# Earlier and wider spaced x sums, half-width k-v products and a split last output in a fused linear-attention and bilinear-GLU kernel

## The chip, the cores and the metric

The kernel runs on one core of one Trainium2 chip. The metric is the device time of one execution in microseconds (us). One execution was also profiled: its instructions, waits and transfers are what the profile and the trace below show. The engines are called as the profile calls them: PE (matmuls) with PEld (weight loads), DVE, ACT, POOL, and SP, whose queue issues most of the transfers.

## The reference

Two branches read the same input `x` (2048 x 512) and are mixed by a gate per row:

```python
x = A_x
g = _sigmoid((x * gate_w).sum(-1, keepdims=True))
# linear attention, 32 heads of 16, phi(t) = (t > 0 ? t + 1 : exp(t)) + 1e-6
q, k, v = split(x @ wqkv)
kv  = einsum("bhsd,bhse->bhde", phi(k), v);  z = phi(k).sum over s
a   = (einsum(phi(q), kv) / (einsum(phi(q), z) + 1e-6)) @ wo
# bilinear GLU, 1792 hidden columns
b   = ((x @ w_gate) * (x @ w_up)) @ w_down
return g * a + (1 - g) * b
```

## The kernel before, in words

**Numbers in two parts.** Every fp32 operand is split into a high part (rounded to the type fp32r) and a low part (the rest). A product is three matmuls, high x high, high x low and low x high (`mm3`, L73). The splits cost ACT (the high parts, `act`) and DVE (the low parts, `tt`) one pass each.

**First stage.** Sixteen tiles of 128 rows are turned into phi(k), and x^T phi(k) is summed in four PSUM banks (`gt`), which `g_evac` (L786) copies out as `gts`.

**Second stage.** 2048 columns of x^T are worked in two pairs of 1024 columns (`NPAIR` = 2). A pair has 16 units: two for q (`q0`, `q1`) and 14 for the GLU. The products of a unit are done with seven half-size products in place of eight (Strassen's scheme, with Winograd-like sums), so a unit is seven slots of six matmuls each; slot s of unit n has the number 7n + s, and the first unit starts at 81.4 us of the span. The seven products need sums of blocks of x (`xc`, one for each of the products 1 to 7, table `SUMS` at L166) and sums of blocks of the weights (`wr`, loaded by `w_load` through SP, added up by `w_add`: two ACT copies and an accumulating transfer issued by POOL).

**What is hung on slots.** `later(slot, fn)` puts a step behind the product of a slot, and `unit` (L649) calls in each slot: the product, the evacuations that wait, the steps of that slot, the weight steps (`side`), the seeding of the next PSUM bank, the links of the Strassen sums (`crit`), and a down-projection job. Each engine works its own instructions strictly in the order in which they were recorded, and so do the queues of SP and POOL. An instruction at the head that waits, waits for all behind it.

**The sums for the second pair.** For i = 3, 4, 1, 6, 7 and two halves k, `x_raw` (L753) loads a block of 256 KB by SP into a work buffer `xw`; `x_sum` (L757) negates it on ACT where the sum is a difference (i = 3 and 4, so four times), then adds another block by an accumulating transfer that POOL issues; `x_park` (L760) writes the sum to a scratch `xpark` in memory by SP, for which the accumulation must have landed; `x_free` (L763) gives the buffer back. At the turn between the pairs `x_turn` loads the parked sums into `xc`. Work buffers come from a list of 45, first in first out (`get`, `put`), so a change of the order of `get` also changes which buffer each later step has.

**The k-v products.** `kv_unit` (L794), in slot 16, multiplies `wv` by `gts` in plain fp32: for each of four blocks b of 128 columns, four products of 128 x 128 by 128 columns, summed in the PSUM bank `pkv`. Each such product leaves two weight loads and two matmuls in the trace. Only the 16 x 16 blocks on the diagonal are wanted: `kv_split` (L803), slot 18, multiplies the bank by a mask (`kvm`), and splits the result.

**The end of a pair.** `turn` (L975) runs eight jobs of six pieces (18 matmuls, `piece`, L958) in which the attention output and the rest of the down-projection are summed in a bank `pdn`; `done` (L945) adds the bank to the accumulator tile `M` on DVE and stores `M` in `out`. Three PSUM banks are shared in turn by these jobs. The last steps on `M` (`steps`, L584) are hung on pieces by their offset, piece p having offset 14 + p.

Of the kernel before, what the change touches and what calls it, by code (L numbers as in the profile page):

```python
# [42 lines left out]
def gated_mix(ctx: ExitStack, tc, xt, xp, x, wqkv, wq, wq_add, wo, wgu, wgu_add, wdn, wdn_add, wdl, gate_w, out):  # L43
# [6 lines left out]
    def mm(*args, **kw):  # L50
        tc.keep_in_program_order(nc.tensor.matmul(*args, **kw))  # L51
# [7 lines left out]
    def tt(dst, a, b, op):  # L59
        pin(nc.vector.tensor_tensor(dst, a, b, op=op))  # L60
# [125 lines left out]
    def get(name):  # L186
        k = spare.pop(0)
        w = p2.tile([P, CH], F32R, tag=f"w{k}", name=name)
        held[id(w)] = (k, w)
        return w  # L190
# [5 lines left out]
    def f32(w):  # L196
        return w.bitcast(F32)
# [4 lines left out]
    def job_bank():  # L202
        return bank_of("pd", "pdn", 3)
# [285 lines left out]
    class Group:  # L489
# [50 lines left out]
        def plain(self):  # L540
# [27 lines left out]
            def add(a, b, d, op, free):  # L568
                m = macc[b, d]
                tt(f32(macc[a, d]), f32(macc[a, d]), m if b == STAYS else f32(m), op)  # L570
                if free and b != STAYS:
                    put(macc.pop((b, d)))
# [11 lines left out]
            def steps(off, *fns):  # L584
                for k, fn in enumerate(fns):
                    if pair == NPAIR - 1 or off + k < 14 + TURN[0]:
                        when(min(off + k, 13 + TURN[pair]), fn)
                    else:
                        later(7 * units * (pair + 1) + (off + k - 14 - TURN[0]) // 2, fn)
# [6 lines left out]
            for d in range(2):  # L596
                steps(39 + 3 * d, lambda d=d: add(2, 4, d, ALU.add, False), lambda d=d: scale(2 + d, 0))
            for d in range(2):
                steps(50 + 6 * d, lambda d=d: add(7, 1, d, ALU.add, False), lambda d=d: add(7, 4, d, ALU.add, True),
                      lambda d=d: scale(d, 0))  # L600

        def seed(self, i, d):
# [175 lines left out]
    def wp_load():  # L778
# [4 lines left out]
        for k in range(KT):  # L783
            dma(f32(att["wo"][k]), wo[k * P:(k + 1) * P, :])

    def g_evac():  # L786
        att["g"] = [get("gts") for _ in range(KT)]
        for d in range(KT):
            if d % 2:
                act(f32(att["g"][d]), accs[d])  # L790
            else:
                pin(nc.vector.tensor_copy(f32(att["g"][d]), accs[d]))

    def kv_unit():  # L794
        pkv = psum.tile([P, KT, P], F32, tag="pd", name="pkv", bufs=3)
        for b in range(KT):
            sl = slice(b * P, (b + 1) * P)
            for d in range(KT):
                mm(pkv[:, b], f32(att["wv"][d])[:, sl], f32(att["g"][d])[:, sl], start=d == 0, stop=d == KT - 1)
        att["pkv"] = pkv  # L800
        put(*att["wv"], *att["g"])

    def kv_split():  # L803
        kvm, hi, lo = get("kvm"), get("kvh"), get("kvl")
        tt(blocks(f32(kvm)), att["pkv"], bmask[:, None, :].to_broadcast([P, KT, P]), ALU.mult)
        act(hi, f32(kvm))
        tt(lo, f32(kvm), f32(hi), ALU.subtract)
        put(kvm)
        att["kvm"] = [hi, lo]
# [131 lines left out]
    def ends_jobs(pair):  # L941

        gr = groups[pair * NG + NG - 1]

        def done(d, c, bank):  # L945
            w = c_tile(d, c)
            tt(f32(w), f32(w), bank, ALU.add)
            col = (2 * pair + c) * CH
            to = nc.gpsimd if pair == 0 else nc.sync
            pin(to.dma_start(out[d * P:(d + 1) * P, col:col + CH], f32(w)))  # L950
            if pair == 0:
                later(now_slot[0] + 8, lambda: put(w))

        for c in 1, 0:
            for n, d in enumerate(half[c]):
                box = {}

                def piece(k, c=c, n=n, d=d, box=box):  # L958
                    sl = slice(d * P, (d + 1) * P)
                    if k == 0:  # L960
                        box["bank"] = job_bank()
                    if k < KT:
                        w, h = [v[:, sl] for v in wp[k]], os_[k, c]
                    else:
                        w = [v[:, d // 2, (d % 2) * P:(d % 2 + 1) * P] for v in dcs[gr.g, k - KT + 1]]
                        h = gr.ops[("12", "22")[k - KT] if c else ("11", "21")[k - KT]]
                    mm3(box["bank"], w, h, k == 0, k == KT + 1)
                    if n == 3:
                        put(*(os_.pop((k, c)) if k < KT else h))
                    if k == KT + 1:  # L970
                        waiting.append(lambda: done(d, c, box["bank"]))

                queue.extend(lambda k=k, piece=piece: piece(k) for k in range(KT + 2))
# [25 lines left out]
    for p in range(NPAIR):  # L999
        last = 7 * (units * (p + 1) - 1)  # L1000
        for k, s in enumerate((-3, -1, 0, 2)):
            later(last + s, lambda k=k: o_split(k, 1))
    later(14, g2_load)
    later(15, g_evac)
    later(16, kv_unit)
    later(18, kv_split)
# [4 lines left out]
    for i in 2, 5:  # L1011
        later(20, lambda i=i: dma(xpark[i], xp[1, SUMS[i][1]]))
    for n, (i, k) in enumerate((i, k) for i in (3, 4, 1, 6, 7) for k in range(2)):
        later(48 + 5 * n, lambda i=i, k=k: x_raw(i, k))
        later(53 + 5 * n, lambda i=i, k=k: x_sum(i, k))
        later(59 + 5 * n, lambda i=i, k=k: x_park(i, k))
        later(62 + 5 * n, lambda i=i, k=k: x_free(i, k))
    later(4, lambda: d_add(0))
    later(4, wp_load)
    for n, (pair, kind, m) in enumerate(order):  # L1020
# [62 lines left out]
```

## Time and profile before

| what | value |
|---|---|
| time, median of 3 runs | 598.98 us (596.04 to 599.48) |
| the profiled execution's own time | 596.77 us |
| its span, first to last instruction | 594.7 us (2.07 us lie around it) |
| mean granted PE clock | 1.000 |
| busy share PE / PEld / DVE / ACT / POOL | 98 / 81 / 84 / 69 / 10 % |
| bytes moved | 95.55 MB, mean 161 GB/s |

Times in the quoted lines are microseconds from the start of the span, unless they are durations; where a group of instructions is listed, ns are means or minimum/median/maximum. A line of a timeline gives start, duration, engine, source line, operation, output<-inputs, shape and count, and in brackets the idle time of the engine before it and what ended that. A line of waits says who waited for whom, the total, how often, and the longest. A line of windows gives a stretch, its length, the busy time of PE, PEld, DVE, ACT and POOL in it (with the number of instructions), the granted clock, the busy share of the 16 DMA engines, and the GB/s. `L57` is the helper `act`, `L60` the helper `tt`, `L51` the helper `mm`, `L81` and `L84` the helpers that issue transfers on SP and accumulating ones on POOL; groups are told apart by their tiles.

### The profile page before, as it was taken

Reading aid. Unit: us, or ns where it says so; the run is one execution under the profiler, and the core shown is the slowest. Engines: PE = TensorE matmul, PEld = TensorE weight load, DVE = VectorE, ACT = ScalarE, POOL = GpSimd, SP = SyncE. Lnnn points to the kernel's source line nnn. Section 1 sums busy time; section 2 is a strip of 40 time slices with the busy share of each in tenths; the row PEclk is TensorE's granted clock in tenths of the full one; section 3 lists DMA queues with packets and bytes.
Section 4 is the critical chain, followed back from the end, with each engine's and each line's share of the span. In section 5 each row is a group of like instructions: output and inputs, shape, how many; then the busy total and the mean of one; then the engine's idle time right before and its main releaser. Section 6 shows DMA issues by size and latency. Waiting matters only on the chain.

```text
span 594.7 us, 7760 instructions
## 1 busy us (share of the span) xinstructions
PE 585.7 (98%) x2579; PEld 479.4 (81%) x2579; DVE 501.2 (84%) x809; ACT 408.7 (69%) x734; POOL 61.2 (10%) x79
## 2 busy tenths in 40 slices
PE   8999999999999989999999999999999999999997
PEld 6888888888778777888878888888887888888885
DVE  6969967777898989897999976969899999799873
ACT  3858957668987777787773664888686878777300
POOL 0041000010011112111101100201010101000000
PEclk9999999999999999999999999999999999999999
DMA  8699567594584989796778447837857665431011
GB/s 301 212 191 301 128 204 160 129 269 97 126 209 116 217 214 235 169 240 149 189 213 230 117 113 196 180 107 152 209 112 165 163 144 128 86 83 33 0 72 71
DMA packets 44185, 95.55 MB, mean 161 GB/s; under 512 B 4305, under 2 KB 13521, under 8 KB 44113
## 3 DMA queue, kind: packets, MB, share of 16 engines
q0 software_dynamic: 9856, 36.18, 33.7%
q1 hardware_dynamic: 34144, 58.62, 30.2%
q8 instruction: 20, 0.33, 0.2%
q10 hardware_dynamic: 144, 0.26, 0.1%
q14 instruction: 21, 0.16, 0.1%
HBM read 83.76 MB, written 12.34 MB: 162 GB/s over the span
## 4 chain that ended last, share of the span: by engine, by line
PE 85%; DVE 7%; ACT 3%; DMA 3%; issue 2%; DVEq 0%; ACTq 0%
PE pdn L51 24%; PE bR L51 12%; PE bY L51 12%; PE bX L51 12%; PE pk L51 7%; PE gt L51 7%; PE bS L51 6%; PE pM L51 3%; DMA wr<-in_wgu 2%; DVE wcl L60 1%; DVE M L60 1%; DVE c L60 1%; DVE hl L60 1%; DVE t L60 1%; PE pkv L51 1%
## 5 line engine op out<-in xcount | busy, mean ns | idle before, releaser
L60 DVE TENSOR_TENSOR wcl<-wr,wch 128x512 fp32r<-128x512 f32 (+1 forms) x96 | 74.2, 773 | 2.0 <-ACT wch L57 2.0
L51 PE MATMUL pdn<-hh,dh 128*128 128x512 f32 x176 | 68.9, 392 | 1.8 <-ACT pdn L57 1.8
L51 PE MATMUL pdn<-hl,dh 128*128 128x512 f32 x176 | 68.5, 389 | 0.0
L51 PE MATMUL pdn<-hh,dl 128*128 128x512 f32 x176 | 68.5, 389 | 0.0
L60 DVE TENSOR_TENSOR M<-M,pdn 128x512 f32<-128x512 f32 x76 | 52.0, 684 | 19.2 <-PE pdn L51 19.2
L57 ACT ACTIVATE wch<-wr 128x512 fp32r<-128x512 f32 (+1 forms) x96 | 66.8, 698 | 0.0
L57 ACT ACTIVATE M<-pdn 128x512 f32<-128x512 f32 x84 | 50.3, 599 | 12.8 <-PE pdn L51 10.0
L57 ACT ACTIVATE hh<-c 128x512 fp32r<-128x512 f32 x56 | 35.3, 630 | 31.0 <-DVE c L60 31.0
L84 POOL DMA_DIRECT2D wr<-in_wgu_add x28 | 24.2, 864 | 295.2 <-ACT wr L57 166.1
L51 PE MATMUL bX<-xbh,wch 128*128 128x512 f32 x128 | 49.8, 389 | 0.0
L51 PE MATMUL bX<-xbl,wch 128*128 128x512 f32 x128 | 49.8, 389 | 0.0
L51 PE MATMUL bX<-xbh,wcl 128*128 128x512 f32 x128 | 49.8, 389 | 0.0
L51 PEld LDWEIGHTS pdn<-hh,dh 128*128 128x128 f32 x176 | 33.0, 188 | 10.2 <-ACT pdn L57 3.4
L60 DVE TENSOR_TENSOR hl<-c,hh 128x512 fp32r<-128x512 f32 x56 | 38.4, 687 | 2.2 <-ACT hh L57 1.9
L51 PEld LDWEIGHTS pdn<-hh,dl 128*128 128x128 f32 x176 | 33.0, 188 | 6.9
L57 ACT ACTIVATE wr<-wr 128x512 f32<-128x512 f32 x64 | 36.7, 625 | 2.5 <-DMA wr<-in_wgu 2.3
L51 PEld LDWEIGHTS pdn<-hl,dh 128*128 128x128 f32 x176 | 33.0, 188 | 6.6
L57 ACT ACTIVATE c<-bX 128x512 f32<-128x512 f32 x28 | 16.8, 600 | 30.7 <-DVE bS L60 30.7
L57 ACT ACTIVATE pdn<-M 128x512 f32<-128x512 f32 x60 | 35.5, 592 | 0.0
L57 ACT ACTIVATE m<-bY 128x512 f32<-128x512 f32 x32 | 19.0, 593 | 21.0 <-PE bY L51 17.3
L60 DVE TENSOR_TENSOR dl<-dr,dh 128x512 fp32r<-128x512 f32 (+1 forms) x40 | 29.6, 766 | 1.9 <-ACT dh L57 1.8
L60 DVE TENSOR_TENSOR t<-bR,c 128x512 f32<-128x512 f32 x32 | 22.0, 687 | 8.5 <-PE bR L51 7.6
(186 smaller groups left out, 1591.6 us busy)
## 6 DMA issues: line engine op xcount, KB each, us to landing
wr<-in_wgu_add POOLq DMA_DIRECT2D x28, 640.0 KB, 6.6
wr<-in_wgu SPq DMA_DIRECT2D x28, 384.0 KB
dr<-in_wdn_add POOLq DMA_DIRECT2D x12, 640.0 KB, 8.3
dr<-in_wdn SPq DMA_DIRECT2D x12, 384.0 KB
xraw<-in_x SPq DMA_DIRECT2D x16, 256.0 KB
terms<-zq SPq DMA_DIRECT2D x16, 256.0 KB
zt<-terms SPq DMA_DIRECT2D x16, 256.0 KB
rb<-den SPq DMA_DIRECT2D x16, 256.0 KB
```

The costliest lines, as they stand in the source:

```text
L51: tc.keep_in_program_order(nc.tensor.matmul(*args, **kw))
L57: pin(nc.scalar.activation(dst, src, func, **kw))
L60: pin(nc.vector.tensor_tensor(dst, a, b, op=op))
L84: tc.keep_in_program_order(nc.gpsimd.dma_start(dst, src, accum_op=ALU.add))
```

## The change

Four things change.

1. The last steps of the second pair on the accumulator tile of product 7 (two additions and a scaling, for d = 0 and 1) move from offsets 50 to 52 and 56 to 58 to offsets 45 to 50.
2. The k-v products are done for the two 64 x 64 quarters on the diagonal of each block alone: 32 products of 128 x 64 by 64 columns in place of 16 of 128 x 128 by 128. The two quarters of a block use different halves of the array's columns (`tile_position=(0, e)`, e = 0 or 64) and come right behind each other. The mask product is done in two instructions of 64 partitions, and the tile it writes is cleared by POOL in slot 12.
3. The ten x sums of the second pair start at slot 14 instead of 48 and come every 8 slots instead of every 5. Within a sum the distances stay: load, 5 slots to the sum, 6 to the store, 3 to the release.
4. For the very last product, ACT copies the accumulator tile into the PSUM bank first, and the matmuls add to it; then DVE copies out the first half of the columns, ACT the second, and each half is stored by a transfer of its own, by SP and by ACT's queue.

```diff
@@ class Group, plain
-                steps(50 + 6 * d, lambda d=d: add(7, 1, d, ALU.add, False), lambda d=d: add(7, 4, d, ALU.add, True),
+                steps(50 + 6 * d if pair < NPAIR - 1 else 45 + 3 * d, lambda d=d: add(7, 1, d, ALU.add, False), lambda d=d: add(7, 4, d, ALU.add, True),
@@
+    def kv_zero():
+        att["kv0"] = get("kvm")
+        pin(nc.gpsimd.memset(f32(att["kv0"]), 0.0))
@@ kv_unit
-            sl = slice(b * P, (b + 1) * P)
             for d in range(KT):
-                mm(pkv[:, b], f32(att["wv"][d])[:, sl], f32(att["g"][d])[:, sl], start=d == 0, stop=d == KT - 1)
+                for e in (0, P // 2):
+                    sl = slice(b * P + e, b * P + e + P // 2)
+                    mm(pkv[e:e + P // 2, b, e:e + P // 2], f32(att["wv"][d])[:, sl], f32(att["g"][d])[:, sl],
+                       start=d == 0, stop=d == KT - 1, tile_position=(0, e))
@@ kv_split
-        kvm, hi, lo = get("kvm"), get("kvh"), get("kvl")
-        tt(blocks(f32(kvm)), att["pkv"], bmask[:, None, :].to_broadcast([P, KT, P]), ALU.mult)
+        kvm, hi, lo = att.pop("kv0"), get("kvh"), get("kvl")
+        for e in (0, P // 2):
+            sl = slice(e, e + P // 2)
+            tt(blocks(f32(kvm))[sl, :, sl], att["pkv"][sl, :, sl],
+               bmask[sl, None, sl].to_broadcast([P // 2, KT, P // 2]), ALU.mult)
@@ ends_jobs, done
+            if (pair, d, c) == very_last:
+                mid = CH // 2
+                pin(nc.vector.tensor_copy(f32(w)[:, 0:mid], bank[:, 0:mid]))
+                act(f32(w)[:, mid:], bank[:, mid:])
+                dma(out[d * P:(d + 1) * P, col:col + mid], f32(w)[:, 0:mid])
+                pin(nc.scalar.dma_start(out[d * P:(d + 1) * P, col + mid:col + CH], f32(w)[:, mid:]))
+                return
@@ ends_jobs, piece
+                        if seeded:
+                            act(box["bank"], f32(c_tile(d, c)))
...
-                    mm3(box["bank"], w, h, k == 0, k == KT + 1)
+                    mm3(box["bank"], w, h, k == 0 and not seeded, k == KT + 1, seeded)
@@
+    later(12, kv_zero)
...
-        later(48 + 5 * n, lambda i=i, k=k: x_raw(i, k))
+        later(14 + 8 * n, lambda i=i, k=k: x_raw(i, k))
...
```

Three places show how instructions move. The first is SP's queue from slot 13 to slot 28, before; `xpark<-in_xp` are the two sums that need no adding, `wr` the weights of a later unit, `dr` those of the down-projection, `terms`, `zt` and `den` belong to the attention's denominators.

```order
L81 DMA g<-gates 32x1x128 x8
L81 DMA zt<-terms_897 128x512 x4
L81 DMA dr<-in_wdn 128x768
L81 DMA xpark_889<-in_xp 16x8192
L81 DMA xpark_893<-in_xp 16x8192
L81 DMA wr<-in_wgu 128x768
L81 DMA den_898<-den 4x32x128
L81 DMA wr<-in_wgu 128x768
```

The same place now:

```order
L81 DMA g<-gates 32x1x128 x8
L81 DMA xw<-in_xp 128x512
L81 DMA zt<-terms_897 128x512 x4
L81 DMA dr<-in_wdn 128x768
L81 DMA xpark_889<-in_xp 16x8192
L81 DMA xpark_893<-in_xp 16x8192
L81 DMA wr<-in_wgu 128x768
L81 DMA xw<-in_xp 128x512
L81 DMA xpark_890<-xw 128x512
L81 DMA den_898<-den 4x32x128
L81 DMA wr<-in_wgu 128x768
```

Two loads of a sum and one store of a sum (which waits for an accumulation issued by POOL) now stand among these transfers; the store has `den` and a weight load behind it.

The second place is ACT's order in slots 34 to 36, before (`hh`, `dh` are high parts of the down-projection's operands, `m` is the copy of a bank that the next product's bank `bR` needs):

```order
L57 ACTIVATE wph<-pdn 128x512
L57 ACTIVATE hh<-c_1569 128x512
L57 ACTIVATE dh<-dr 128x768
L57 ACTIVATE m_1669<-bY 128x512
L57 ACTIVATE hh<-ts 128x512
```

and now:

```order
L57 ACTIVATE wph<-pdn 128x512
L57 ACTIVATE hh<-c_1598 128x512
L57 ACTIVATE dh<-dr 128x768
L57 ACTIVATE xw<-xw 128x512
L57 ACTIVATE m_1701<-bY 128x512
L57 ACTIVATE hh<-ts 128x512
```

The third of the four negations stands right ahead of `m`. 

The third place is ACT's end now, with the engine or queue whose semaphore each instruction waits for in brackets. Before, the list ended with the `oh` rows.

```order
L57 ACTIVATE oh<-phq 128x512
L57 ACTIVATE oh<-phq 128x512 [waits DVE_49] x2
L57 ACTIVATE oh<-phq 128x512 [waits PE_49]
L57 ACTIVATE pdn<-M 128x512 [waits DVE_49]
L57 ACTIVATE M<-pdn 128x256 [waits DVE_49]
L962 DMA out<-M 128x256 [waits DMAHW7_49,Activation_49]
```

The copy of the second half waits for DVE: the value it waits for is that of DVE's copy of the first half, so the two copies come one after the other.

More of the change, by code (lines that the diff above doesn't have):

```diff
@@ L946, in done @@
             w = c_tile(d, c)
+            col = (2 * pair + c) * CH
+            if (pair, d, c) == very_last:
[5 more added lines that the diff above has]
+                return
             tt(f32(w), f32(w), bank, ALU.add)
-            col = (2 * pair + c) * CH
             to = nc.gpsimd if pair == 0 else nc.sync
@@ L952, in done @@
                 later(now_slot[0] + 8, lambda: put(w))
+        very_last = (NPAIR - 1, half[0][-1], 0)
         for c in 1, 0:
@@ L959, in piece @@
                     sl = slice(d * P, (d + 1) * P)
+                    seeded = (pair, d, c) == very_last
                     if k == 0:
                         box["bank"] = job_bank()
+                        if seeded:
+                            act(box["bank"], f32(c_tile(d, c)))
                     if k < KT:
@@ L1013, in gated_mix @@
     for n, (i, k) in enumerate((i, k) for i in (3, 4, 1, 6, 7) for k in range(2)):
-        later(48 + 5 * n, lambda i=i, k=k: x_raw(i, k))
-        later(53 + 5 * n, lambda i=i, k=k: x_sum(i, k))
-        later(59 + 5 * n, lambda i=i, k=k: x_park(i, k))
-        later(62 + 5 * n, lambda i=i, k=k: x_free(i, k))
+        later(14 + 8 * n, lambda i=i, k=k: x_raw(i, k))
+        later(14 + 5 + 8 * n, lambda i=i, k=k: x_sum(i, k))
+        later(14 + 11 + 8 * n, lambda i=i, k=k: x_park(i, k))
+        later(14 + 14 + 8 * n, lambda i=i, k=k: x_free(i, k))
     later(4, lambda: d_add(0))
```

## The prediction

> **What bounds the kernel now.** The page's first and fourth parts come first: how long each engine is busy, and which engine the chain that ended last runs through.
>
> ```profile
> PE 585.7 (98%) x2579; PEld 479.4 (81%) x2579; DVE 501.2 (84%) x809; ACT 408.7 (69%) x734; POOL 61.2 (10%) x79
> PE 85%; DVE 7%; ACT 3%; DMA 3%; issue 2%; DVEq 0%; ACTq 0%
> ```
>
> PE works 585.7 of 594.7 us and carries 85% of the chain. So only three things can move the time: PE's own work, the 9.0 us in which it idles, and new waits. The waits of PE say what the idle time is:
>
> ```profile
> PE pdn L51 <- ACT pdn L57: 1.8, 1, 1.8
> PE warm L51 <- DVE xc1h L108: 1.3, 1, 1.3
> PE bR L51 <- DVE t L60: 0.7, 2, 0.5
> PE bY L51 <- ACT m L57: 0.3, 1, 0.3
> ```
>
> 1.3 us lie ahead of the first matmul, which the change doesn't touch. One wait, of 1.8 us, stands out. The chain around it, in order of time, and ACT's row there:
>
> ```profile
> 196.57 11.57 DMA wr<-in_wgu
> 208.17 1.15 ACT wr L57 x2
> 209.32 0.50 ACT pdn L57
> 208.17 1.15 ACT L57 ACTIVATE wr<-wr 128x512 f32<-128x512 f32 x2 [1.58 <-DMA wr<-in_wgu]
> ```
>
> A weight load took 11.57 us to land. ACT stood 1.58 us at the head of its queue for it, and the seed of a PSUM bank (`pdn`) that PE needed was queued behind. Why the load was slow is seen in the windows and in what POOL issued just before:
>
> ```profile
> 120.00:140.00 20.00, 19.96 (x89) 16.20 (x88) 17.03 (x29) 13.70 (x27) 2.44 (x3) 1.00 0.87 220
> 140.00:160.00 20.00, 19.66 (x87) 15.68 (x86) 14.74 (x24) 18.40 (x35) 0.86 (x1) 1.00 0.51 128
> 160.00:180.00 20.00, 19.77 (x88) 16.02 (x87) 19.07 (x31) 16.68 (x31) 2.58 (x3) 1.00 0.72 172
> 200.00:220.00 20.00, 18.18 (x81) 14.71 (x80) 17.77 (x30) 14.23 (x27) 2.58 (x3) 1.00 0.94 231
> 220.00:240.00 20.00, 20.00 (x88) 15.97 (x87) 19.88 (x33) 15.95 (x30) 4.35 (x5) 1.00 0.91 225
> 192.60 0.86 POOL L84 DMA_DIRECT2D wr<-in_wgu_add  x1 [13.12 <-PE pdn L51]
> 193.91 0.86 POOL L84 DMA_DIRECT2D xw<-in_xp  x1 [0.44 <-ACT xw L57]
> 196.72 0.86 POOL L84 DMA_DIRECT2D dr<-in_wdn_add  x1 [1.95 <-DVE wcl L60]
> 204.59 0.86 POOL L84 DMA_DIRECT2D xw<-in_xp  x1 [7.01 <-ACT xw L57]
> ```
>
> The DMA engines are 94% busy in that stretch, with four accumulations in 12 us, two of them x sums (`xw`). In the same windows PE idles in no other by more than 0.34 us.
>
> **Part 3, the x sums.** The same ten loads, ten accumulations, ten stores and four negations are issued; only their places change. Slots last about 2.1 us, so a sum every 8 slots is one per 17 us where it was one per 10.5.
>
> *What goes.* Around the slow load (slots 52 to 59) the accumulations were in slots 53 and 58; they will be in 51 and 59, so one has left before the weights' own accumulation and the other comes when the load is due. But a store falls in slot 57 that was not there, so the relief is not whole. Bounds: nothing, or all of the 1.8 us. I take 1.5, as 1.58 us earlier landing in 11.57 is all that is needed. When this stall goes, the next of PE's waits are under 0.7 us.
>
> *What comes: negations.* ACT runs them in its queue:
>
> ```profile
> L57 ACT ACTIVATE xw<-xw x4: 617/622/627, 193.0 to 228.4; 128x512 f32<-128x512 f32 x4
> 157.55 0.83 ACT L57 ACTIVATE dh<-dr 128x768 fp32r<-128x768 f32 x1
> 158.28 0.58 ACT L57 ACTIVATE m<-bY 128x512 f32<-128x512 f32 x1
> 158.91 0.50 PE L51 MATMUL bY<-xc4h,wch 128*128 128x512 f32 x1 [0.34 <-ACT m L57]
> 131.25 1.15 ACT L57 ACTIVATE wr<-wr 128x512 f32<-128x512 f32 x2 [0.18 <-DMA wr<-in_wgu]
> 139.47 0.60 ACT L57 ACTIVATE ex<-bX 128x512 f32<-128x512 f32 x1 [1.84 <-DVE bS L60]
> ```
>
> The third negation (slot 35) now stands between `dh` and `m` at 158 us, where PE already waits for `m`. It takes some 0.5 us of ACT (rows overlap at their ends: the pair of 0.62 us `wr` copies spans 1.15), and all of it is PE's: +0.5 us. The first, second and fourth lie where ACT later idles (1.84 us at 139.47) and cost nothing; without that idle time each would cost up to 0.5. ACT waits in these places for the sum's load; it is issued five slots (10 us) ahead, which covers a landing like the accumulations' here:
>
> ```profile
> DMA to landing us min/median/max: 6.1/7.9/10.1
> 126.03 0.35 SPq L81 DMA_DIRECT2D wr<-in_wgu  x1
> 141.25 0.63 SPq L81 DMA_DIRECT2D den<-den  x1
> 127.86 0.86 POOL L84 DMA_DIRECT2D dr<-in_wdn_add  x1 [7.13 <-ACT dr L57]
> ```
>
> *What comes: queues and bandwidth.* On SP the store of the first sum now stands ahead of `den` and of a weight load. Its accumulation follows `dr` on POOL, at about 128.7, and lands 7.9 us later, at 136.6. `den` was not issued before 141.25, so the store holds up nobody; were it to land over 4.6 us late, the weight load behind it would be late by the excess. POOL's queue gets the accumulation right behind `dr` too, ahead of weight sums that wait for ACT anyway. Bandwidth is the dearer point: the weight load issued at 126.03 was already awaited by ACT (0.18 us at 131.25), in a stretch that is 87% busy, and now 256 KB of load follow right behind it and a 256 KB accumulation starts at 128.7. At 220 GB/s those 512 KB are 2.4 us if the load had to wait for all, and nothing if it goes ahead. ACT then has 1.84 us to catch up, so PE loses between 0 and 0.6 us directly, up to 2.4 if the copies behind are urgent. I take 0.3, nearer the low end, because the load is ahead in its queue.
>
> **Part 2, the k-v products.** Their matmuls and weight loads, beside the loads of the only other plain fp32 products, `pz`, which move 2 columns where these move 128:
>
> ```profile
> 116.19 3.83 PE L51 MATMUL pkv<-gts,wv 128*128 128x128 f32 x32
> 115.97 3.86 PEld L51 LDWEIGHTS pkv<-gts,wv 128*128 128x128 f32 x32
> L51 PEld LDWEIGHTS pkv<-gts,wv x32: 186/192/192, 116.0 to 119.6; 128*128 128x128 f32 x32
> 95.29 1.08 PEld L51 LDWEIGHTS pz<-ones,zacc 128*128 128x128 f32 x8
> ```
>
> The pace of the loads is (3.86 - 0.19) / 31 = 0.118 us with 128 columns moving, and (1.08 - 0.19) / 7 = 0.127 us with 2. So the loading of 128 columns of weights sets the pace, not the columns that move, and halving the moving columns alone gains nothing. The 32 new products should leave 64 loads of half the columns. If a load's time goes with its columns and loads follow each other, that is 64 x 0.059 = 3.8 us, no change from 3.8. If the two column halves load side by side, it is 1.9 us, a gain of 1.9. If the pace per load stays at 0.118 whatever its size, it is 7.6 us, a loss of 3.8. I take 2.6 us, a gain of 1.2, since consecutive products go to different halves. The trace of before has no such product, so all three ends stay in the range.
>
> On this the Trainium skill speaks both ways (TensorEngine Tiling (Array Packing), section Tiling Modes): tiles of the array load weights and multiply in parallel, which would be the 1.9 us, but a change of the tiling mode drains the engine, here once ahead of these products and once behind. No run here shows either; by that page the term would be the 1.9 us gain less two drains.
>
> The mask product on DVE becomes two instructions of 256 elements per partition:
>
> ```profile
> 122.12 0.68 DVE L60 TENSOR_TENSOR kvm<-pkv,bmask 128x512 f32<-128x512 f32 x1
> 202.17 0.42 DVE L60 TENSOR_TENSOR zt<-zt 128x256 f32<-128x256 f32 x1
> ```
>
> 2 x 0.42 - 0.68 = +0.2 us of DVE, ahead of the subtraction for `bS`; I count all of it (bounds 0 and 0.2). POOL's clearing of a tile in slot 12 is one memset on an engine that is 10% busy; nothing. That PE is sooner done only helps if ACT and DVE keep up: ACT was busy 18.40 of 20 us in the next windows and DVE 19.07 of 20, which is why I don't take the whole 1.9.
>
> **Parts 1 and 4, the end.** The last DVE row and the windows behind it:
>
> ```profile
> 590.57 0.69 DVE L60 TENSOR_TENSOR M<-M,pdn 128x512 f32<-128x512 f32 x1 [2.06 <-PE pdn L51]
> 591.26:592.20 0.94, 0.00 (x0) 0.00 (x0) 0.00 (x0) 0.00 (x0) 0.00 (x0) 1.00 0.06 26
> 592.20:593.30 1.10, 0.00 (x0) 0.00 (x0) 0.00 (x0) 0.00 (x0) 0.00 (x0) 1.00 0.56 216
> 593.30:594.70 1.40, 0.00 (x0) 0.00 (x0) 0.00 (x0) 0.00 (x0) 0.00 (x0) 1.00 0.00 0
> ```
>
> From DVE's end at 591.26 to the end of the span are 3.44 us, of which the bytes take about 1.1. Now DVE copies half (0.42, as the 256-element row), to 590.99. ACT's copy waits for DVE's: half of a copy of 0.60 us, by the step from 0.60 to 0.83 us for 256 elements more, is 0.37 us, to 591.36 or 591.40 with the hand-over. Then 3.44 us, less up to 0.55 for half the bytes. The end moves by between +0.15 and -0.4 us; I take -0.1. The seed is an ACT copy of 0.6 us in a stretch in which ACT has nothing else to do, and the steps on the tile now end at offset 50, six pieces (4 us) before the last product starts at offset 56: nothing, while without the earlier steps the seed would have waited until offset 58 and held PE.
>
> **Sum.** -1.5 (slow load) + 0.5 (third negation) + 0.3 (load at 126) - 1.2 (k-v) + 0.2 (mask) - 0.1 (end) = -1.8 us. From the profiled execution's own time, 596.77 (span 594.7 plus 2.07 around it), that is 595.0 us. The median of the three runs, 598.98, is 2.2 us above the profiled one, and no view says what those 2.2 are; I keep them: **597.2 us**, -0.3%.
>
> **Rivals.**
> *The load wait only moves.* All transfers of the sums are still made, the store in slot 57 falls into the slow load, and the load at 126 had no slack before. Then the -1.5 goes and the 0.3 becomes about 1.3: 599.7 us. Against it: one accumulation fewer just ahead of the slow load.
> *Slower: the half-width loads keep the pace of the whole ones.* PE's sequence of k-v products grows from 3.8 to 7.6 us, +3.8 in place of -1.2: 602.2 us. It decides from a pace of 0.059 us per load on; for it speaks that load and matmul come as a pair every 0.12 us in both rows, against it nothing but that column counts should matter.
> *Much faster: halves side by side, and waiting on transfers gone.* -1.9 for k-v, -1.8 for the slow load, no new wait at 126, and the 2.2 us that the usual run has over the profiled one are waits of the same kind and go too: 598.98 - 1.9 - 1.8 - 2.2 + 0.5 + 0.2 - 0.1 = 593.7 us. Against it: PE has few waits outside the one, and one of the three runs, at 596.04, is without the 2.2 anyway. The tiling page's rule in full is this rival's first term.
>
> **How the numbers follow.** Forecast 0.50, load wait moves 0.22, slower 0.15, much faster 0.13. The range is 593.2 to 602.0 us: it holds the forecast (594 to 599 with the bounds of its terms), the first rival and about half of each of the others. About 1%, 6 us, is what a measurement of this kernel can tell from no change; faster than 593.0 is half of the much faster case, 0.07; slower than 605.0 needs the slow pace and a new load wait together, 0.05; within 1% is the rest, 0.88.
>
> **What would show it.** Right: the 1.8 us wait of PE for `pdn` gone, the load near 196 us landing in under 10; the `pkv` group of 64 loads in 2 to 3 us; a longer wait of PE for `m` near 157; the last ACT copy behind DVE's and the span's end some 3 us behind it. Wrong: the `pkv` group at over 5 us; a new ACT wait for `wr` of over 1 us between 120 and 180, with a wait of PE behind it; or PE waits of over 3 us anywhere else.

## The result and the profile after

| | before | after |
|---|---|---|
| median, 22 runs of each beside each other | 596.75 us (595.75 to 599.48) | 598.97 us (597.24 to 601.54) |
| ratio after / before | | 1.0033, 95% interval 1.002 to 1.0046 |
| profiled execution | 596.77 us, span 594.7 us | 599.16 us, span 597.1 us |

The changed kernel is slower by 0.33%, about 2 us, where a gain of 0.3% was forecast. The change is smaller than the spread of single executions, but over 22 of each it is clear: the interval leaves out 1. Its sign was predicted wrongly. In the larger sample before's median is the profiled execution's own time: the 2.2 us that lay between the two in the first three runs are no property of the kernel.

First the page of after, its lines on the busy time of PE and on the chain:

```profile
PE 585.9 (98%) x2611; PEld 478.5 (80%) x2611; DVE 500.9 (84%) x810; ACT 409.5 (69%) x736; POOL 61.6 (10%) x80
PE 86%; DVE 5%; ACT 4%; DMA 2%; issue 2%; DVEq 0%; ACTq 0%
```

PE works as long as before, with 32 matmuls more, and the span is 2.4 us longer. So PE idles 2.4 us more, and its waits say where:

```profile
PE pdn L51 <- ACT pdn L57: 2.0, 1, 2.0
PE bS L51 <- DVE bS L60: 1.5, 2, 1.1
PE warm L51 <- DVE xc1h L108: 1.3, 1, 1.3
PE bR L51 <- DVE t L60: 1.2, 3, 0.5
PE bY L51 <- ACT m L57: 0.9, 1, 0.9
```

The wait for `pdn` that was to go is there (2.0 us, 1.8 before). Two waits for `bS`, of 1.5 us together, are new: 1.1 us at 141.85 us, and 0.4 us at 125 us, right behind the k-v products. Those for `t` and `m` have grown from 0.7 and 0.3.

**The new wait, at 126 to 142 us.** The window of this stretch in after, and of the one with the slow load:

```profile
120.00:140.00 20.00, 19.20 (x84) 15.24 (x83) 15.07 (x26) 13.56 (x26) 3.46 (x4) 1.00 0.98 255
200.00:220.00 20.00, 18.00 (x80) 14.54 (x79) 17.56 (x31) 12.51 (x24) 2.22 (x3) 1.00 0.87 210
```

Between 120 and 140 us the DMA engines are 98% busy (87% before) and move 255 GB/s (220). In before they were full in the first half of this stretch only (a share of 1.00 from 120 to 130 us, 0.75 from 130 to 140); now they stay full to its end (0.94 and 1.01). The timeline of after for SP, POOL, ACT and PE shows the weight load issued at 125.98 there:

```profile
125.98 0.34 SPq L81 DMA_DIRECT2D wr<-in_wgu  x1
126.42 0.44 SPq L81 DMA_DIRECT2D xw<-in_xp  x1
128.50 1.21 POOL L84 DMA_DIRECT2D xw<-in_xp  x1
134.29 1.15 ACT L57 ACTIVATE wr<-wr 128x512 f32<-128x512 f32 x2 [2.60 <-DMA wr<-in_wgu]
138.42 0.50 PE L51 MATMUL bR<-xc6h,wch 128*128 128x512 f32 x1 [0.40 <-DVE t L60]
141.74 0.60 ACT L57 ACTIVATE ex<-bX 128x512 f32<-128x512 f32 x1 [1.09 <-DVE bS L60]
141.85 0.47 PE L51 MATMUL bS<-xah,wch 128*128 128x512 f32 x1 [1.09 <-DVE bS L60]
```

From the issue of the load to ACT's copy of it are 8.3 us (125.98 to 134.29), where it was 5.2 us before (126.03 to 131.25). ACT stood 2.60 us at the head of its queue for it, in place of 0.18. Behind `wr` on ACT stand copies that DVE needs, and DVE works in order too: its `bS`, for which ACT's `ex` waits, came 2.3 us later than before (141.74 against 139.47). PE waited twice.

**The third negation.** ACT and PE at 160 us in after:

```profile
160.43 0.61 ACT L57 ACTIVATE xw<-xw 128x512 f32<-128x512 f32 x1
160.95 0.58 ACT L57 ACTIVATE m<-bY 128x512 f32<-128x512 f32 x1
161.58 0.50 PE L51 MATMUL bY<-xc4h,wch 128*128 128x512 f32 x1 [0.94 <-ACT m L57]
```

The negation starts 0.52 us ahead of `m`, and PE's wait for `m` went from 0.34 to 0.94 us.

**The slow load.** The chain of after there, and SP and POOL in its timeline:

```profile
199.48 11.55 DMA wr<-in_wgu
211.03 0.02 issue
211.06 0.03 ACT wr L57
211.08 0.51 issue
211.59 0.61 ACT wr L57
212.20 0.50 ACT pdn L57
```

```profile
199.90 0.45 SPq L81 DMA_DIRECT2D xpark<-xw  x1
199.62 0.86 POOL L84 DMA_DIRECT2D dr<-in_wdn_add  x1 [3.46 <-DVE wcl L60]
201.50 0.86 POOL L84 DMA_DIRECT2D xw<-in_xp  x1 [1.02 <-DVE c L60]
```

The load takes 11.55 us as before (11.57). A store of a sum was issued 0.42 us behind it, and the accumulation of the sum hung on slot 59 was issued 2.02 us behind it, while the load was under way.

**The k-v products and the end.** The tile `pkv` in after (weight loads), the mask product, and the last instructions:

```profile
L51 PEld LDWEIGHTS pkv<-gts,wv x64: 132/138/138, 117.1 to 119.2; 128*64 128x64 f32 x64
117.12 2.17 PEld L51 LDWEIGHTS pkv<-gts,wv 128*64 128x64 f32 x64 [0.35 <-DVE gts L796]
121.73 0.85 DVE L60 TENSOR_TENSOR kvm<-pkv,bmask 64x256 f32<-64x256 f32 x2
592.74 0.39 PE L51 MATMUL pdn<-hh,dl 128*128 128x512 f32 x1
593.23 0.42 DVE L959 COPY M<-pdn 128x256 f32<-128x256 f32 x1 [3.46 <-PE pdn L51]
593.69 0.38 ACT L57 ACTIVATE M<-pdn 128x256 f32<-128x256 f32 x1 [7.34 <-DVE M L959]
```

64 loads in 2.17 us are (2.17 - 0.14) / 63 = 0.032 us each. The last copy ends at 593.69 + 0.38 = 594.07, 3.0 us ahead of the span's end.

**The accounts of the two profiled executions.** Matmuls of 512 columns start 0.227 us after each other where nothing holds them. What an interval has beyond that (counted where it is over 0.28 us) is lost PE time. By stretch, in us:

| | before | after | difference |
|---|---|---|---|
| start to first k-v matmul | 116.20 | 117.13 | +0.93 |
| first k-v matmul to next product | 3.58 | 2.24 | -1.34 |
| lost from there to 145 us | 0.37 | 2.76 | +2.39 |
| of it ahead of `bS` at 125 us | 0.20 | 0.57 | +0.37 |
| lost, 145 to 200 us | 1.11 | 1.82 | +0.71 |
| lost, 200 to 225 us | 2.09 | 2.28 | +0.19 |
| lost, after 225 us | 2.48 | 2.36 | -0.12 |
| last matmul to end of span | 4.55 | 4.35 | -0.20 |

Together that is +2.56 of 2.4 us (the rest is in intervals under the limit). The first line is hardly the change's doing: the first stage is the same, and its length varies from 116.1 to 118.3 us over the kernels below (see the end). Without it the table gives some 1.5 us, within the 1.2 to 2.7 us that the interval of the ratio allows.

### The profile page after: what moved, and what is told of

The parts are those of the page before. It is cut to its first block, busy times and chain, and to the rows that moved or that the text cites. A ratio compares the mean times of both kernels' runs of the same rounds, so it can differ in the third digit from the quotient of the medians.

```text
span 597.1 us, 7824 instructions
## 1 busy us (share of the span) xinstructions
PE 585.9 (98%) x2611; PEld 478.5 (80%) x2611; DVE 500.9 (84%) x810; ACT 409.5 (69%) x736; POOL 61.6 (10%) x80
## 4 chain that ended last, share of the span: by engine, by line
PE 86%; DVE 5%; ACT 4%; DMA 2%; issue 2%; DVEq 0%; ACTq 0%
PE pdn L51 25%; PE bY L51 13%; PE bR L51 13%; PE bX L51 12%; PE pk L51 8%; PE gt L51 7%; PE bS L51 6%; PE pM L51 2%; DMA wr<-in_wgu 2%; DVE wcl L60 1%; ACT M L57 1%; DVE t L60 1%; DVE M L60 1%; DMA wraw<-in_wqkv 1%; DVE hl L60 1%
## 5 line engine op out<-in xcount | busy, mean ns | idle before, releaser
L57 ACT ACTIVATE M<-pdn 128x512 f32<-128x512 f32 (+1 forms) x85 | 50.8, 598 | 20.3 <-PE pdn L51 9.9
L57 ACT ACTIVATE dh<-dr 128x512 fp32r<-128x512 f32 (+1 forms) x40 | 26.1, 683 | 3.4 <-PE pdn L51 3.4
```

Of the source, the lines that this page charges most:

```text
L57: pin(nc.scalar.activation(dst, src, func, **kw))
```

## The experiments

Two theories stood against each other at first. One: the x sums at their new places delay weight loads for which ACT, and through it PE, then waits; without part 3 the change would gain. Two: the sums cost little, and something in the other parts (the products' two column groups, the mask in two, the zeroed tile) gives the time back. Each ratio is to the kernel before, timed beside it on the same chip in five rounds (`e11` in three); `e1` to `e4`, `e5` to `e8`, `e9` to `e12` and `e13` ran on four different chips, so two experiments of different sets are compared only through their ratios.

**The parts one by one.** `e1_no_sums` is the changed kernel with the sums at their old places:

```diff
-        later(14 + 8 * n, lambda i=i, k=k: x_raw(i, k))
+        later(48 + 5 * n, lambda i=i, k=k: x_raw(i, k))
...
```

> The changed kernel with the x sums put back to slot 48 + 5n (parts 1, 2 and 4 stay). Theory: the earlier sums are the whole loss, and the other parts gain what the two profiles show (k-v products 1.3 us, the end 0.2 us): 1.5 us faster than before, about 595.2 us. Rival: the loss lies in the other parts (the seeded bank, two queues at the end, a longer start at the low clock): 1 to 2 us slower than before. The slow weight load near 196 us, with ACT's wait for it of about 1.6 us, should be there in both.

`e2_sums_alone` is the kernel before with part 3 alone (the diff of `e1` the other way round):

```diff
-        later(48 + 5 * n, lambda i=i, k=k: x_raw(i, k))
+        later(14 + 8 * n, lambda i=i, k=k: x_raw(i, k))
...
```

> The kernel before with part 3 alone (sums at slot 14 + 8n). Theory: about 3.3 us slower than before, about 600.0 us: an ACT wait of 2 to 3 us for the weight load issued near 126 us, with 2 us of PE waits behind it until 142 us, and 0.6 us more at the third negation near 160 us. Rival (loss elsewhere): within 1 us of before.

`e3_kv_alone` is before with part 2 alone:

```diff
+    later(12, kv_zero)
...
-                mm(pkv[:, b], f32(att["wv"][d])[:, sl], f32(att["g"][d])[:, sl], start=d == 0, stop=d == KT - 1)
+                for e in (0, P // 2):
+                    sl = slice(b * P + e, b * P + e + P // 2)
...
```

> The kernel before with part 2 alone (k-v products by quarters). Theory: 1.3 us faster than before, about 595.4 us, with 64 matmul records of pkv in 2.2 us. Rival: what PE gains there it waits for later, because ACT and DVE are nearly full until 180 us: within 0.4 us of before.

`e4_end_alone` is before with parts 1 and 4 alone:

```diff
+            if (pair, d, c) == very_last:
+                mid = CH // 2
+                pin(nc.vector.tensor_copy(f32(w)[:, 0:mid], bank[:, 0:mid]))
...
```

> The kernel before with parts 1 and 4 alone (earlier last steps, last bank seeded, copied and stored by halves). Theory: 0.2 us faster than before: last matmul to end of span 4.35 us instead of 4.55. Rival: nothing, or slower by up to 0.2 us if ACT's queue starts its transfer later than SP's.

Measured: `e1` 0.9993 (0.998 to 1.0006), `e2` 1.0018 (0.9994 to 1.0041), `e3` 0.9997 (0.9977 to 1.0017), `e4` 1.0002 (0.9989 to 1.0015). So part 3 makes the difference: with it the other parts are at 1.0033, without it at 0.9993, 2.4 us less, and the two intervals lie apart. By itself, in `e2`, part 3 costs less, 1.1 us, and its interval includes 1. Neither of the other parts gains anything that can be seen by itself, the k-v products included, although they take 1.34 us less of PE in `e3`.

`e2` did not do what was expected at 126 us: ACT's wait for the weight load was 0.90 us, not 2 to 3, and PE lost almost nothing there although the DMA engines were full. Its window, and then SP's and ACT's rows for the load, first of `e1`, then of `e2`:

```profile
120.00:140.00 20.00, 19.96 (x91) 16.29 (x91) 15.93 (x27) 13.87 (x27) 3.46 (x4) 1.00 1.01 262
```

```profile
124.91 0.35 SPq L81 DMA_DIRECT2D wr<-in_wgu  x1
131.55 1.16 ACT L57 ACTIVATE wr<-wr 128x512 f32<-128x512 f32 x2 [1.59 <-DMA wr<-in_wgu]
126.66 0.35 SPq L81 DMA_DIRECT2D wr<-in_wgu  x1
133.12 1.16 ACT L57 ACTIVATE wr<-wr 128x512 f32<-128x512 f32 x2 [0.90 <-DMA wr<-in_wgu]
```

In `e1`, with the sums at their old places, the load is issued 1.1 us sooner than before (126.03) but reaches ACT no sooner (131.55, 131.25 before). The four kernels side by side, each cell with the time from issue to ACT's copy, ACT's wait for the load, and PE's loss from the k-v products to 145 us (as in the accounts above), in us:

| | sums at the old places | sums early |
|---|---|---|
| k-v products whole | before: 5.2, 0.18, 0.37 | `e2`: 6.5, 0.90, 0.56 |
| k-v products by quarters | `e1`: 6.6, 1.59, 1.11 | after: 8.3, 2.60, 2.76 |

So each change alone lengthens the load by 1.2 to 1.4 us, both together by 3.1, and only both together cost PE over 2 us there. Early sums also change which buffer each step has; but the load is not issued later by that: it comes 9.84 us behind the first k-v matmul in before and in `e2`, and 8.85 and 8.86 us behind it in `e1` and after. These are single profiles, but others agree: `e4` repeats the first cell (5.2, 0.20, 0.36), and `e9` and `e12` below, which have no early sums, the third (6.7 in both; 1.65 and 1.63; 1.18 and 1.16). `e3`, the k-v products alone, does not fit it: there another load, that of `dr`, was late. ACT's row in its timeline:

```profile
128.56 1.15 ACT L57 ACTIVATE dr<-dr 128x512 f32<-128x512 f32 x2 [2.63 <-DMA dr<-in_wdn]
```

ACT took this tile at 126.41 us in before, without a wait, so the load was not only not earlier but later. In this profile PE lost 2.95 us up to 145 us, against 0.37 before. It is one of the longer executions of `e3` (598.42 us; the twelve run from 595.66 to 599.56, median 597.67), so it does not show what the median run loses.

**The two big copies.** In slot 20, two copies of 512 KB (`xpark[2]` and `xpark[5]`) are issued in the crowded stretch. If the stretch is short of DMA time, moving them should help as much as moving the sums. `e5_copies_late` does that in the changed kernel, `e6_kv_copies_late` in `e1`, `e7_before_copies_late` in the kernel before. The edit of all three:

```diff
-    for i in 2, 5:
-        later(20, lambda i=i: dma(xpark[i], xp[1, SUMS[i][1]]))
+    for i, s in (2, 84), (5, 94):
+        later(s, lambda i=i: dma(xpark[i], xp[1, SUMS[i][1]]))
```

> The changed kernel with one edit: the two 512 KB copies of x into the scratch (products 2 and 5), which stood in slot 20, stand in slots 84 and 94. Theory: the loss, and the k-v gain that never showed, come from ACT waiting for dr and wr loads in a stretch, 117 to 142 us, where the DMA engines are full; without these 1 MB both waits go, PE's waits between 124 and 142 us fall from 2.3 us to under 0.5, and the kernel is about 2 us faster than the changed one, 596.5 to 597 us. Rival: the accumulation and the load of the first sums slow the weight load whatever else moves: the ACT wait stays at 2 us or more and the time within 0.7 us of the changed kernel.

> Parts 1, 2 and 4 (sums at slot 48 + 5n) with the two 512 KB copies moved to slots 84 and 94. Theory: the k-v products' gain of 1.3 us is kept, since no load is late when PE arrives early: 1.3 to 2 us faster than before, about 595.5 us, with no ACT wait for dr or wr between 122 and 142 us. Rival (the gain is lost to ACT and DVE being nearly full until 180 us, not to loads): within 0.5 us of before.

> The kernel before with only the two 512 KB copies moved to slots 84 and 94. Theory: before had no PE wait between 124 and 142 us beyond 0.3 us, so there is nothing to win: within 0.5 us of before. Rival: the copies cost something of their own in before (through later loads): over 0.7 us faster.

Measured: 1.0021 (1.0 to 1.0042), 0.9998 (0.9975 to 1.0022), 1.0004 (0.9985 to 1.0023). None of the three differs clearly from its own kernel with the copies early. In `e5` ACT no longer waited for `wr`, but 0.95 us for `dr`, and PE still lost 1.79 us up to 145 us. The window of `e5`:

```profile
120.00:140.00 20.00, 19.60 (x86) 15.44 (x84) 15.85 (x27) 14.06 (x27) 3.46 (x4) 1.00 0.98 222
```

The copies are gone from 120 to 140 us and 222 GB/s are moved in place of 255, yet the DMA engines are as busy. So with the sums early the engines stay full without the copies. Where the sums are not early, the share does fall with the copies, from 0.87 in before to 0.82 in `e7`.

**The sums late.** `e8_sums_late` has parts 1, 2 and 4, and keeps the sums out of both crowded places: none before slot 62, then one every 4 slots, and the copies in slots 30 and 36.

```diff
-        later(14 + 8 * n, lambda i=i, k=k: x_raw(i, k))
+        later(62 + 4 * n, lambda i=i, k=k: x_raw(i, k))
...
-    for i in 2, 5:
-        later(20, lambda i=i: dma(xpark[i], xp[1, SUMS[i][1]]))
+    for i, s in (2, 30), (5, 36):
+        later(s, lambda i=i: dma(xpark[i], xp[1, SUMS[i][1]]))
```

> Parts 1, 2 and 4 with the sums at slots 62 + 4n and the two copies in slots 30 and 36, so that no transfer of the sums is left between 185 and 205 us. If the sums' accumulations make the weight load issued near 197 us slow (as the prediction had it), it lands in under 9 us, ACT's wait of 1.6 us goes and PE gains about 2 us, unless denser sums after 210 us cost new waits. If it is the weights' own accumulations and the denominators' loads, it takes 11 us as before and PE's 1.8 us wait stays.

Measured: 0.9958 (0.9939 to 0.9977), 595.04 us; it beats both kernels. The windows of `e8` and, behind them, PE's waits for `pdn`:

```profile
120.00:140.00 20.00, 19.60 (x87) 15.93 (x86) 17.75 (x30) 14.16 (x28) 2.57 (x3) 1.00 0.82 176
200.00:220.00 20.00, 19.49 (x87) 15.80 (x86) 18.91 (x32) 14.92 (x28) 0.86 (x1) 1.00 0.62 159
```

```profile
PE pdn L51 <- ACT pdn L57: 0.5, 2, 0.3
```

With no transfer of a sum near 196 us the load lands before ACT asks for it, and the gap of PE near 208 us shrinks from 2.4 to 0.9 us; it is now a wait for `t`. The two waits for `pdn` in the line are others, at 233.10 and 307.84 us, behind the denser sums: after 225 us PE loses 3.24 us, 0.8 more than before, which is part of the price of this placing. In the stretch from 120 us the DMA engines are 82% busy, ACT waits for no load, and PE loses 0.76 us up to 145 us in place of 2.76.

Is it the sums or the copies? `e9_sums_late_copies_early` is `e8` with the copies back in slot 20, and `e10_before_sums_late` is the kernel before with the sums and copies placed as in `e8`, without parts 1, 2 and 4:

```diff
-    for i, s in (2, 30), (5, 36):
-        later(s, lambda i=i: dma(xpark[i], xp[1, SUMS[i][1]]))
+    for i in 2, 5:
+        later(20, lambda i=i: dma(xpark[i], xp[1, SUMS[i][1]]))
```

> Parts 1, 2 and 4 with the sums at slots 62 + 4n, and the two 512 KB copies left in slot 20. If the late sums alone took away the slow weight load near 197 us, this is as fast as with the copies moved, about 2.5 us (0.4%) faster than before, with no PE wait of over 1 us near 208 us. If the copies in slots 30 and 36 were half of it, it is within 0.2% of before.

```diff
-        later(48 + 5 * n, lambda i=i, k=k: x_raw(i, k))
+        later(62 + 4 * n, lambda i=i, k=k: x_raw(i, k))
...
```

> The kernel before with the sums at slots 62 + 4n and the copies in slots 30 and 36, and none of the change. Its distance to the same placing with parts 1, 2 and 4 (0.9958 of before) is what these parts are worth when no load is late: 1.2 us or 0.2% by the PE records (k-v 1.3 less 0.4 at the next bS, end 0.2), so about 0.998 of before. Rival: the parts are worth nothing, and this is 0.996.

Measured: `e9` 0.9972 (0.9953 to 0.9991), `e10` 0.9983 (0.9969 to 0.9997). The late sums alone bring the gain at 208 us (0.78 us lost from 200 to 225 in `e9`, as in `e8`). From `e10` to `e8` is 0.0025, or 1.5 us: what parts 1, 2 and 4 seem to be worth where no load is late, against 0.0007 in the old places (`e1`). The intervals of `e8` and `e10` just overlap, and the two ran on different chips; `e9`, on the chip of `e10` but with the copies early, is only 0.0011 below it. So the size is not sharp.

**The negation.** `e11_negation_behind` moves the third negation by one slot, behind `m`:

```diff
-        later(14 + 5 + 8 * n, lambda i=i, k=k: x_sum(i, k))
+        later(14 + 5 + (n == 2) + 8 * n, lambda i=i, k=k: x_sum(i, k))
```

> The changed kernel with the third negation one slot later (36), so that ACT copies m first. The gap of PE near 160 us (1.33 us between two matmuls in all profiles with early sums, 0.74 in those without) falls back to about 0.75 us; the time falls by 0.5 to 0.6 us, to about 1.0024 of before. Rival: ACT is full there and the gap stays at over 1.1 us.

Measured: 1.0035 (1.001 to 1.0059), no gain. The timeline of `e11`:

```profile
160.25 0.50 PE L51 MATMUL bY<-xc4h,wch 128*128 128x512 f32 x1 [0.41 <-ACT m L57]
166.75 0.50 PE L51 MATMUL bR<-xc6h,wch 128*128 128x512 f32 x1 [0.76 <-DVE t L60]
```

PE's wait for `m` fell from 0.94 to 0.41 us, and the wait for `t` that follows rose from 0.25 to 0.76. From 145 to 200 us PE lost 1.78 us, against 1.82. Half a microsecond more of ACT work in this stretch cost PE half a microsecond at both places that were tried.

**Which sums.** `e12_sums_31_7` leaves the changed kernel as it is but starts the sums at slot 31, one every 7 slots: none in the crowded stretch, and other neighbours for the load at 196 us.

```diff
-        later(14 + 8 * n, lambda i=i, k=k: x_raw(i, k))
+        later(31 + 7 * n, lambda i=i, k=k: x_raw(i, k))
...
```

> The changed kernel with the sums at slots 31 + 7n: no transfer of the sums before 145 us, and the negations behind m. If crowding between 117 and 142 us and the negation ahead of m are the whole loss, it is as the changed kernel with the sums put back, 0.9993 of before. If sums that overlap the attention's transfers cost time wherever they stand before slot 60, it stays at 1.002 or more, with PE waits at other places.

Measured: 0.9982 (0.9967 to 0.9998). Up to 145 us PE lost 1.16 us (after: 2.76, `e1`: 1.11), from 145 to 200 us 1.68, and from 200 to 225 us 0.75. At the last place ACT's row in `e12` shows a short wait:

```profile
207.78 1.16 ACT L57 ACTIVATE wr<-wr 128x512 f32<-128x512 f32 x2 [0.36 <-DMA wr<-in_wgu]
```

So the relief of the load at 196 us can be had with another placing: PE loses 0.75 us there where before lost 2.09, 1.3 us less and near the 1.5 that was forecast. The load takes 10.1 us there (197.65 to 207.78). A store of a sum stands 0.42 us behind it as in after, but the next accumulation of a sum is issued 6.80 us behind it (204.45) in place of 2.02, which points to the accumulation more than to the store.

What was open then was whether the two first sums alone make the loss, or the other eight have a part in it. `e13_first_two_early` is `e12` with only the first two sums back in slots 14 and 22, where the changed kernel has them:

```diff
-    for n, (i, k) in enumerate((i, k) for i in (3, 4, 1, 6, 7) for k in range(2)):
-        later(31 + 7 * n, lambda i=i, k=k: x_raw(i, k))
+    starts = (14, 22, 45, 52, 59, 66, 73, 80, 87, 94)
+    for s, (i, k) in zip(starts, ((i, k) for i in (3, 4, 1, 6, 7) for k in range(2))):
+        later(s, lambda i=i, k=k: x_raw(i, k))
...
```

> The kernel with the sums at slots 31 + 7n (0.9982 of before), with one edit: the first two sums go back to slots 14 and 22, where the changed kernel has them; the other eight stay, so no negation stands ahead of m and the load near 197 us has what it had. If the crowd between 117 and 142 us is the loss, an ACT wait for dr or wr loads of over 2 us comes back there with 1 to 2 us of PE waits until 142 us, and the time goes to 1.001 or more of before (over 1.5 us slower than with 31 + 7n). If not, it stays at 0.998 to 0.999, and the loss lay in the spacing by 8 or in the negations.

Measured: 1.0008 (0.9991 to 1.0025), 0.0026 or 1.5 us above `e12` and just short of the 1.001 that was expected. The two intervals overlap, so by time alone this is likely rather than certain. In the trace of `e13` ACT waits 3.30 us for the load of `dr` that was issued in the crowded stretch. Timeline of ACT, and windows:

```profile
128.86 1.15 ACT L57 ACTIVATE dr<-dr 128x512 f32<-128x512 f32 x2 [3.30 <-DMA dr<-in_wdn]
```

```profile
120.00:140.00 20.00, 18.04 (x69) 13.59 (x68) 14.24 (x24) 13.39 (x26) 3.25 (x4) 0.91 1.00 257
133.50:136.80 3.30, 3.30 (x10) 2.59 (x9) 3.30 (x6) 3.30 (x8) 0.86 (x1) 0.55 1.02 194
```

The DMA engines are full (share 1.00, 0.98 in after). This is another load than the one that was late in after, and `e3` and `e6` wait for it too (2.63 and 2.69 us) without early sums. So this profile does not show that the first two sums made it late; it fits them, and no more.

**All kernels side by side.** Lost PE time is counted as above, in one profiled execution of each, so the ratio decides. Some of these executions are not typical of their kernel: those of `e3`, `e6`, `e7` and `e10` took 598.42, 599.18, 599.34 and 598.10 us, 0.8 to 2.7 us more than the medians (597.67, 596.45, 597.18 and 596.16).

| kernel | to first k-v | k-v | lost to 145 | 145 to 200 | 200 to 225 | after 225 | ratio |
|---|---|---|---|---|---|---|---|
| before | 116.20 | 3.58 | 0.37 | 1.11 | 2.09 | 2.48 | 1 |
| after | 117.13 | 2.24 | 2.76 | 1.82 | 2.28 | 2.36 | 1.0033 |
| `e1` no sums moved | 116.07 | 2.23 | 1.11 | 1.14 | 3.79 | 2.58 | 0.9993 |
| `e2` sums alone | 116.83 | 3.58 | 0.56 | 1.75 | 1.82 | 2.29 | 1.0018 |
| `e3` k-v alone | 116.58 | 2.24 | 2.95 | 1.09 | 2.09 | 2.60 | 0.9997 |
| `e4` end alone | 116.68 | 3.58 | 0.36 | 1.17 | 1.63 | 2.60 | 1.0002 |
| `e5` after, copies late | 117.11 | 2.23 | 1.79 | 1.79 | 2.00 | 2.40 | 1.0021 |
| `e6` `e1`, copies late | 116.80 | 2.23 | 3.02 | 1.15 | 2.29 | 3.15 | 0.9998 |
| `e7` before, copies late | 117.10 | 3.58 | 0.37 | 1.14 | 3.78 | 2.56 | 1.0004 |
| `e8` sums from 62 | 116.68 | 2.24 | 0.76 | 1.11 | 0.78 | 3.24 | 0.9958 |
| `e9` same, copies early | 116.69 | 2.24 | 1.18 | 1.09 | 0.78 | 3.24 | 0.9972 |
| `e10` before, sums from 62 | 118.33 | 3.58 | 0.37 | 1.09 | 0.73 | 3.22 | 0.9983 |
| `e11` negation behind | 116.46 | 2.23 | 2.57 | 1.78 | 2.12 | 2.40 | 1.0035 |
| `e12` sums from 31 | 117.05 | 2.24 | 1.16 | 1.68 | 0.75 | 2.40 | 0.9982 |
| `e13` first two early | 116.21 | 2.24 | 4.72 | 1.18 | 0.90 | 2.19 | 1.0008 |

From `e1` to after, part 3 costs 2.76 - 1.11 = 1.65 us up to 145 us and 1.82 - 1.14 = 0.68 us up to 200 us. That is 2.3 of the 2.4 us between their ratios. (The 3.79 of `e1`, the 3.78 of `e7` and the 4.72 of `e13` each hold 1.7 us of matmuls at half the clock, which is told at the end.)

Two things stay open. One is why the load of `dr` lands late in some kernels and not in others with the same transfers: ACT waited 2.6 us for it in the profile of `e3` and did not in that of `e1`, and in `e6`, where there is less to transfer, it waited 2.7 us. With one profile of each, chance and cause aren't told apart there. The other is how the sums delay a load. That it comes of full DMA engines is argued from the windows; `e2` has full engines and loses hardly any PE time there, so the share alone does not decide.

## Why the prediction failed, step by step

- **The slow load (-1.5): failed.** It became +0.2, 1.7 us of the miss. The prediction took slots for times. It placed the accumulation of slot 59 where "the load is due", and it was issued 2.02 us after the load, at 201.50 us, while the product of slot 59 started at 207.18. A step's slot sets its place in its queue. This sum needs no negation, so POOL did not wait for ACT as it did for the sums of before; its row shows a wait of 1.02 us, for DVE, and it ran ahead of the slot's product. The store in slot 57, which the prediction had seen, was issued 0.42 us behind the load. The size of the term was nearly right, as `e12` and `e8` show with other placings (1.3 us less loss from 200 to 225 us than before).
- **The weight load at 126 us (+0.3): mis-sized.** Behind the `bS` at 125 us and up to 145 us PE lost 2.19 us, 1.8 of them in two gaps, against 0.17 in before. These 2.0 us more are within the bound of 2.4, and they are another 1.7 us of the miss: with the measured values of these two terms the sum of -1.8 would have been +1.6, which is what the accounts give without their first line. "The load is ahead in its queue" was no protection: the time from its issue to ACT's copy grew by 3.1 us, 1.6 to 1.7 of them with the sums behind it (after against `e1`, `e9` and `e12`). The other 1.4 came with the k-v products, as `e1` has them without early sums; the sum of the prediction had no term for two changes that meet at one load. The slack of 1.84 us that was set against it was ACT's. The delay ran through DVE, whose `bS` came 2.3 us later.
- **The third negation (+0.5): right.** 0.6 us at the place named; `e11` adds that it cost the same one place further on.
- **The k-v products (-1.2): right on PE, but not in the time.** They took 1.34 us less: 0.032 us is about a quarter of 0.118, as if two column halves loaded side by side. What the sum left out is that the stretch behind waits for a transfer that PE's speed does not hasten: in `e1` it was issued 1.1 us sooner and reached ACT at the same time. The tiling rule in the Trainium skill, TensorEngine Tiling (Array Packing), section Tiling Modes, that different tiles load and multiply in parallel, fits these runs. The drains at a change of mode, of which it speaks, are small here: PE's interval ahead of the group was 0.32 us for 0.23 in before, and from its last matmul to the next product 0.15 us for 0.03, each some 0.1 more.
- **The mask (+0.2): right for DVE.** The product grew from 0.68 to 0.85 us; PE's loss ahead of the `bS` behind it grew by 0.37 us. The other 0.2 us of this are not explained.
- **The end (-0.1): right**, -0.20.
- **The base (+2.2): failed.** 2.2 us were carried from the median of three runs; over 22 runs the median is the profiled time. This hid part of the error: the predicted change was -1.8 us and the measured one +2.2, and the forecast time is only 1.8 us below the measured one.

Of the rivals, "the load wait only moves" is what happened, with the load at 126 costing 2.0 us where it was given 1.3. That its time (599.7 us) came near is in part luck: its terms add up to +0.7 us, where +2.2 was measured, and the other 2.2 are the base. The slow pace of half-width loads is ruled out by the `pkv` group; "much faster" had the k-v products nearly right and the waits on transfers wrong. Of its own signs, the prediction named the right one as a refutation: a new wait of ACT for `wr` of over 1 us between 120 and 180 us with a wait of PE behind it.

## What to carry to other kernels

Before a transfer is moved, look at the busy share of the DMA engines in the stretch where it will *run* (in its queue, not by its slot), and at which load an engine there stands waiting for at the head of an in-order queue: a stretch at 87% with a load awaited for 0.18 us had room for two more sums (`e2` lost 0.19 us there) or for shorter k-v products ahead of it (`e1`, 0.74 us, the mask's wait included), but not for both (2.39 us). Time saved on PE ahead of such a stretch was in part given back there; it seems to be kept where the loads have slack (`e8` against `e10`). So two changes that lean on the same load have to be added up at that load and not each by itself. Read a slack from every engine that the delay runs through, not from the one that waits first.

## What the runs showed of the hardware that was not expected

**PE at half speed after a wait of some 2 us.** In `e1`, behind the gap near 208 us (2.31 us between two starts), the next eight matmuls start 0.427 us after each other in place of 0.227. Windows of `e1`:

```profile
207.00:213.00 6.00, 4.08 (x11) 2.93 (x10) 4.47 (x8) 3.79 (x7) 0.86 (x1) 0.72 0.81 184
```

The granted clock is 0.72 in this stretch: the trace has it at 0.5 for 3.41 us. The gap thus cost 1.7 us more than itself. The same happened in `e7` at that place, and in `e13` near 134 us behind two gaps of 1.5 and 0.5 us of idle time (the second of its windows above, clock 0.55), each time for 3.41 us. It did not in before, after or `e11`, whose gaps near 210 us were 2.2 to 2.4 us long. So in some executions, not in all, a wait of 2 us cost nearly twice its length. The Trainium skill, TensorE: Matmul & The Clock Gate, section HAM oscillation — how this bites in real kernels, puts the danger at idle gaps of over about 3.4 us; these runs show it at 2.1 us of idle time (2.31 less the usual 0.227), and here the measurement decides. The same page of the Trainium skill, section What's actually happening, calls the window by which the clock is set free-running; that would fit a fall that comes in some executions only, which these runs can't prove.

**The start varies.** The last matmul at the slow pace of 0.427 us at the start comes at 3.4 us in before and at 8.6 us in `e10`, and the first k-v product at 116.2 and 118.3 us, though all kernels begin alike. Two single profiles can differ by a microsecond or two from this alone; it is 0.93 us between those of before and after.
